# When twelve weight stores and one fraction are issued: chunked attention, Fourier mixing and an MLP in fp32

## The chip, the cores and the metric

The kernel runs on one core of a Trainium2 chip. Time is device time in microseconds from one execution; the median over runs is given. A core has five engines that work side by side: TensorE (matrix products, "PE"), VectorE ("DVE"), ScalarE ("ACT"), GpSimd ("POOL") and SyncE ("SP"), which here only issues transfers. Each engine takes its instructions in the order in which the program emits them and waits on semaphores for what other engines and transfers deliver.

## The reference

For 8 batches of 576 tokens and 8 heads of 64, attention is computed within chunks of 64 tokens; the heads are then joined to rows of 512, mixed with the real part of a two-dimensional Fourier transform, normalised, and sent through an MLP with 2048 hidden channels.

```python
scores = scale * np.matmul(q_c, k_c.transpose(0, 1, 2, 4, 3))   # per chunk of 64
attn = np.exp(scores - np.max(scores, axis=-1, keepdims=True))
attn = attn / (np.sum(attn, axis=-1, keepdims=True) + 1e-09)
out = np.matmul(attn, v_c)
x = out.transpose(0, 2, 1, 3).reshape(B, S, H * D)

X = np.fft.fft(np.fft.fft(x, axis=1), axis=2)
u = x + np.real(X).astype(np.float32)
un = (u - mean(u)) / np.sqrt(var(u) + 1e-06)                    # per row of 512
ch = np.maximum(un @ w_ch1, 0.0) @ w_ch2                        # 512 -> 2048 -> 512
return (u + ch).astype(np.float32)
```

q, k and v are float32. The two weights are float64 numbers, 8 bytes each.

## The kernel before

**Tiles and groups.** The tokens of a batch are cut into tiles of 128 rows (a low and a mirrored high tile per pair of chunks) and a rest. Four tiles of a batch make a group; the rests of all batches make the last. The kernel goes through the groups one by one: `mlp(g)` is the MLP of group g, and it yields after every small portion of matmuls. The main loop counts these steps as `t`. Between two steps it puts in portions of the attention and the Fourier mixing of the next batch (`side(b)`, spread over the steps between the times in `ready_at`), and everything else that has to be done by then. So the order of each engine's queue is that in which this loop emits instructions. Group 0 takes the steps 1 to 32: 16 steps up (512 to 2048, line 1219), and 16 down (2048 to 512, line 1260). From group 1 on, the products use fewer, precombined blocks (lines 1309 and 1363; the last two groups line 1427).

**Weights.** There are 32 pieces of 128x512 numbers: 16 of the first weight, into `wa`, and 16 of the second, into `wb`. A piece arrives as raw 8-byte numbers (512 KB, `load_weight`, line 348, issued on SP's queue) in one of a few raw spaces, which lie in `yall` and in rows of `xall`. Later on only three such spaces are left, so that a load waits until an earlier piece has been read. The conversion to float32 is written out by hand in `round_weight(i)`. It works on two pieces at once, the head of piece i and the tail of piece i - 1:

- head: VectorE takes the exponent bits (372) and the upper fraction bits (382). ScalarE makes the fraction, a number from 1 to 2 (`fraction`, line 364), and in two steps the power of two (`exponent` 367, `power_` 370).
- tail: VectorE adds the lower bits to the fraction (379), sets the sign on the power (380), and multiplies both (388). After 380 the raw space is free, and the next load is issued.

With `later` given, the three ScalarE steps are not emitted at once but put into a list, in the order fraction, exponent, power. Piece 1 is handled so: `fourier_early` calls `round_weight(1, put_off, "h")`, and `put_off[0]`, `[1]` and `[2]` are its three steps.

**The first rows.** `fourier_early` mixes the first batch. After the products of line 928 it emits the first two of the put-off steps. Then, for four tiles, VectorE adds the mixed rows (952, 955) and takes their statistics (705, 706). ScalarE makes the inverse deviation (709, 710), and for the first two tiles the normalised rows (996 to 998); VectorE makes those of the other two (1000). TensorE turns the rows (`turned`, line 399), ScalarE copies them to `unT` (1013), and `columns` multiplies them with piece 0 (944). The third put-off step stands after the second tile's turn. The first product with piece 1 is the first of line 1219.

**Stores for later groups.** Groups from 1 on read their weights from blocks kept in DRAM (`s1` and `s2`). Of the second weight, `keep2_whole(i)` stores three unchanged blocks of 256 KB each (line 1114, SP's queue, four calls, so twelve stores), and `keep2(i)` has GpSimd make four sums (line 1095), which go first into rows of `xall` or into `yall` and are stored from there (line 1107). The rows of `xall` are those of the raw spaces. Of the first weight, `keep1_store` (1082) stores blocks as well. All these stand in SP's queue with the loads of the weights and of q, k and v (252, 265, 275).

The loop emits the calls of `keep2_whole` when the pieces that they read have been converted (`n_w` is the number of the next piece):

```python
while n_whole < HF // 2 and n_w > KF + HF + 2 * n_whole + 2:
    keep2_whole(n_whole)
    n_whole += 1
```

Here KF is 16, HF is 8 and `ready_at[0]` is 27.

**The Fourier rows of batch 1** are made in the steps from 20 on (`fourier(1)`): products z on TensorE (722, 732), ScalarE's copies (747, 761), then `round_next()` and only after it `z_joined` on VectorE (752, 756), ScalarE's copies into `zf` (773 to 778), products `mix` (840), VectorE's sums (850, 851), the addition to x (857, on GpSimd for the high tiles), statistics, and the normalised and turned rows for group 1.

Of the kernel before, what the change touches and what calls it, by code (L numbers as in the profile page):

```python
# [11 lines left out]
ALU = mybir.AluOpType  # L12
# [4 lines left out]
def kernel(  # L17
# [32 lines left out]
    nc = tc.nc  # L50
# [10 lines left out]
    KF = DFF // 128  # L61
# [41 lines left out]
    NO, HF = 7, KF // 2  # L103
# [235 lines left out]
    def raw(i):  # L339
        return spaces[raws[i]].bitcast(U32).rearrange("p (f r) -> p f r", r=2)  # L340

    def load_weight(i):

        fit = [r for r in free if (i < N_EARLY or r < N_LATE) and (i < N_LAST or r > 1)]
        if i < len(pieces) and fit:
            raws[i] = fit[0]
            free.remove(fit[0])
            nc.sync.dma_start(out=raw(i).rearrange("p f r -> p (f r)"), in_=pieces[i][1].bitcast(U32))

    def round_weight(i, later=None, parts="ht"):  # L350

        head, tail = "h" in parts and i < len(pieces), "t" in parts and 0 < i <= len(pieces)
        if head:
            w, t = pieces[i][0], raw(i)
            hi, wi = t[:, :, 1], w.bitcast(U32)  # L360
            p = power[i] = three_p.tile([128, 512], U32, tag="o", name="power")

            def fraction(w=w, wi=wi):
                nc.scalar.activation(out=w, in_=wi, func=ACTF.Copy, scale=2.0 ** -20, bias=1.0)

            def exponent(p=p):
                nc.scalar.activation(out=p, in_=p, func=ACTF.Relu, scale=-1.0, bias=top[:, 0:1])

            def power_(p=p):
                nc.scalar.activation(out=p, in_=p, func=ACTF.Relu, scale=-8.0, bias=top[:, 1:2])  # L370

            nc.vector.tensor_scalar(p, hi, 0x7FF00000, None, ALU.bitwise_and)
            if later is None:
                exponent()
                power_()
        if tail:
            w_, t_ = pieces[i - 1][0], raw(i - 1)
            p_ = power.pop(i - 1)
            nc.vector.scalar_tensor_tensor(w_, t_[:, :, 0], 2.0 ** -52, w_, ALU.mult, ALU.add)
            nc.vector.scalar_tensor_tensor(p_, t_[:, :, 1], 0x80000000, p_, ALU.bitwise_and, ALU.bitwise_or)  # L380
        if head:
            nc.vector.tensor_scalar(wi, hi, 0x000FFFFF, None, ALU.bitwise_and)
            if later is None:
                fraction()
            else:
                later += [fraction, exponent, power_]
        if tail:
            nc.vector.tensor_tensor(out=w_, in0=w_, in1=p_.bitcast(FP32), op=ALU.mult)

            r = raws.pop(i - 1)  # L390
            if i - 1 + len(spaces) < N_EARLY or r < N_LATE:
                free.append(r)
            load_weight(max(raws, default=i - 1) + 1)
# [476 lines left out]
    def fourier_early():  # L870
# [59 lines left out]
                    start=(T == 0), stop=(T == 2), skip_group_check=True,  # L930
                )
        idle[0] = mid
        for do in put_off[:2]:
            do()
        keep_warm(3)
        yield
        ups = ps_a.tile([128, 2, 512], FP32, tag="att", name="up_a")
# [3 lines left out]
        def columns(s):  # L941

            for m, up in enumerate(first_ups):
                nc.tensor.matmul(
                    out=up[:, s * 128:(s + 1) * 128], lhsT=w1[:, 0, m * 128:(m + 1) * 128],
                    rhs=unTs[0][:, 0, s * 128:(s + 1) * 128], start=(s == 0), stop=False, skip_group_check=True,
                )

        for i in range(NM):
# [13 lines left out]
            if i == 0:  # L963
                normed(0, 1)
                turned(0, 0)
                keep_warm(1)
        put_off[2]()
        put_off.clear()
        columns(1)
        normed(0, 2)  # L970
# [109 lines left out]
    def keep1_store(pair, o):  # L1080
        to = s1[pair, o].rearrange("p (k x) -> p k x", k=2)
        nc.sync.dma_start(out=to, in_=parts1(pair)[o])
# [26 lines left out]
    def keep2_whole(i):  # L1109

        m = 2 * i
        to = s2.rearrange("o p (m e) -> o p m e", m=HF)
        for o, m0, e0 in ((0, m, 0), (4, HF + m, 0), (5, HF + m, HM)):
            nc.sync.dma_start(out=to[o, :, m:m + 2], in_=w2[:, m0:m0 + 2, e0:e0 + HM])
# [338 lines left out]
    def mlp(g):  # L1453

        for h1 in up_halves(g) if g >= first_of[1] else up_plain(g) if g > 0 else up_first():
            yield
        yield from (down_few if g >= FEW else down_halves if g >= first_of[2] else down_plain)(g, h1)

    with tc.manual_schedule():
# [22 lines left out]
        n_w = 2  # L1482
# [3 lines left out]
        def keep_warm(times):  # L1486

            for _ in range(times):
                nc.tensor.matmul(out=idle[0][:, 0:NQ], lhsT=warm[:, 0:128], rhs=warm[:, 0:NQ], start=True, stop=True)

        put_off, first_ups = [], []

        def round_next(later=None):
            nonlocal n_w
            if n_w <= len(pieces):
                round_weight(n_w, later)
                n_w += 1
# [25 lines left out]
        ready_at = [begin[g] + (2 * KF - 5 if g < first_of[2] else 2 * HF + 4) for g in range(NG)]  # L1523
# [12 lines left out]
        n_whole, n_kept, late, rest_ = 0, 0, [], None  # L1536
        conv2 = chain(conv2)
        t = 0
        for g in range(NG):
            for _ in mlp(g):  # L1540
                t += 1
                heavy = False
                for do in late:
                    do()
                late = []
                if t == 8:
                    nc.scalar.copy(tk, early_tk[:, :, :, 0:NE])
                if cur < len(sides):
                    t0 = 3 if cur == 0 else ready_at[cur - 1]
                    t1 = ready_at[cur]  # L1550
                    due = min(sizes[cur], (t - t0) * sizes[cur] // (t1 - t0))
                    if cur == 0:
                        due = late_due.get(t, (t - t0) * sizes[cur] // (t1 - 2 - t0))
                    while done < due:
                        heavy = next(sides[cur], None) or heavy
                        done += 1
                    if t >= t1:
                        for _ in sides[cur]:
                            pass
                        cur, done = cur + 1, 0  # L1560
                while joined:
                    combined(*joined.pop(0))
                if not heavy:
                    round_next(late if t < KF and t % 4 == 3 else None)
                    if t <= 2 or t < KF and t % 4 == 0 or t >= KF + 3:
                        round_next()

                while n_whole < HF // 2 and n_w > KF + HF + 2 * n_whole + 2:
                    keep2_whole(n_whole)
                    n_whole += 1  # L1570
                keep2_store()
                if n_w > len(pieces):
                    for _ in range(3):
                        next(conv2, None)
                if t == begin[1] - 1:
                    for _ in conv2:
                        pass
                    keep2_store()
                if begin[1] < t < begin[1] + 7 and t % 2:
                    keep1((t - begin[1] + 1) // 2)  # L1580
                if t == ready_at[FEW - 1]:
                    rest_ = make_rest()
                if t >= ready_at[FEW - 1]:
                    next(rest_, None)
                if t == begin[FEW] + 2 * HF - 2:
                    for _ in rest_:
                        pass
                    slab3.extend(
                        one_p.tile([128, Z3], FP32, tag=tag, name="more").rearrange("p (m e) -> p m e", m=4)
                        for tag in ("q", "k")  # L1590
                    )
                for _ in range((2, 3, 10, 11, 12, 12, 13, 13, 14, 15).count(t - begin[FEW])):
                    fetch(3)
                for _ in range(2 if t > begin[1] else 0):
                    if put_off:
                        b, t0_, r, o = put_off.pop(0)
                        nc.sync.dma_start(out=out[b, t0_ + 1 - r:t0_ + CH:2, :], in_=o)
                if KF < t <= KF + 4 or KF + 8 <= t < KF + 16:
                    keep1_store(n_kept // 3, (0, 4, 6)[n_kept % 3])
                    n_kept += 1  # L1600
                if begin[1] <= t < begin[1] + KF:
                    keep1_store((t - begin[1]) // 4, (2, 1, 3, 5)[(t - begin[1]) % 4])
                if t in (begin[1] + 9, begin[1] + 13, begin[1] + 16):
                    fetch(2)
                if t == begin[1] + KF:
                    for _ in range(NS1):
                        fetch(1)
# [49 lines left out]
```

## Time and profile before

| what | value |
|---|---|
| time, median of 3 runs | 1063.99 us (1063.61 to 1064.34) |
| profiled execution, its time | 1063.73 us |
| its span | 1061.9 us |
| TensorE busy | 1043.3 us (98%) |
| VectorE busy | 626.5 us (59%) |
| ScalarE busy | 315.5 us (30%) |
| GpSimd busy | 431.9 us (41%) |
| transfers | 219.10 MB, mean 206 GB/s |

The span is the part of the profiled execution between its first and its last instruction. Busy shares are averages over the whole kernel. What a stage is worth is read from the timeline of that stage: an engine's instructions in order of time, with the idle time before a group and what ended it. The chain of waits follows the work that ended last back to what released it, step by step. Where it names an engine other than TensorE, TensorE's work could not begin before that engine's.

### The profile page before, as it was taken

To read this page: it belongs to the slowest core of one execution; us is meant where nothing else is said; L and a number is where in the kernel's file an instruction comes from. 1 tells how busy PE (TensorE), PEld (TensorE's weight loads), DVE (VectorE), ACT (ScalarE), POOL (GpSimd) and SP (SyncE) were. 2 spreads that over 40 slices of the span, in tenths; PEclk is the share of its full clock that TensorE was granted. 3 is DMA by queue.
4 is the path that set the end of the run, shared out by engine and by line. 5 is a ranking of instruction groups with operands and counts; after the bars stand their busy time and mean duration, and the time that the engine had idled before them with its cause. 6 is when DMAs were issued, how large, how long until landed. Compare 5 with 4: busy or idle time off the path is not lost.

```text
span 1061.9 us, 20222 instructions
## 1 busy us (share of the span) xinstructions
PE 1043.3 (98%) x7482; PEld 851.6 (80%) x7482; DVE 626.5 (59%) x1339; ACT 315.5 (30%) x744; POOL 431.9 (41%) x555
## 2 busy tenths in 40 slices
PE   7999999999999999999999999999999999999998
PEld 6645444788888888888888888888888888888887
DVE  4798986974567465664565645745664666443332
ACT  4688573233113311332022312331133103201200
POOL 3410119753425151244134421514252777660282
PEclk9999999999999999999999999999999999999999
DMA  8767675687688447973678357944753759998364
GB/s 169 221 197 213 163 218 199 203 233 230 231 215 230 134 142 214 250 207 108 186 229 223 118 169 231 250 131 155 215 168 102 269 187 353 363 399 279 89 216 142
DMA packets 167088, 219.10 MB, mean 206 GB/s; under 512 B 77228, under 2 KB 111020, under 8 KB 161614
## 3 DMA queue, kind: packets, MB, share of 16 engines
q1 hardware_dynamic: 155978, 211.98, 64.8%
q0 software_dynamic: 9024, 4.91, 2.1%
q8 instruction: 60, 0.98, 0.4%
q10 hardware_dynamic: 1988, 0.92, 0.3%
q14 instruction: 38, 0.31, 0.1%
HBM read 183.61 MB, written 34.08 MB: 205 GB/s over the span
## 4 chain that ended last, share of the span: by engine, by line
PE 79%; DVE 6%; DMA 4%; ACT 3%; POOL 3%; SPq 2%; issue 2%; DVEq 0%; ACTq 0%; POOLq 0%
PE pa L1309 20%; PE pb L1309 15%; PE pb L1363 14%; PE pa L1363 11%; PE dn L1427 7%; PE pt L399 2%; SPq L265 2%; PE mix L840 2%; PE xp L501 2%; PE z L722 1%; DMA xall<-in_moe_w_ch_dram 1%; PE up L1219 1%; PE sc L451 1%; POOL h L1207 1%; POOL part L1156 1%
## 5 line engine op out<-in xcount | busy, mean ns | idle before, releaser
L1309 PE MATMUL pa<-unT,wa 128*128 128x256 f32 x736 | 175.3, 381 | 0.2 <-DVE xall L1317 0.2
L1309 PEld LDWEIGHTS pa<-unT,wa 128*128 128x128 f32 x736 | 138.1, 190 | 19.6 <-DVE xall L1317 0.6
L1309 PE MATMUL pb<-wa 128*128 128x256 f32 x448 | 106.6, 381 | 0.0
L1309 PEld LDWEIGHTS pb<-wa 128*128 128x128 f32 x448 | 84.3, 190 | 11.5
L1363 PE MATMUL pa<-wb,h 128*128 128x256 f32 x384 | 87.2, 380 | 0.0
L1363 PE MATMUL pb<-wb,h 128*128 128x256 f32 x384 | 86.4, 379 | 0.0
L1193 POOL TENSOR_TENSOR h<-h 128x256 f32<-128x256 f32 x48 | 40.8, 858 | 98.2 <-DVE wb L1191 91.6
L1363 PEld LDWEIGHTS pa<-wb,h 128*128 128x128 f32 x384 | 71.8, 190 | 9.7
L1363 PEld LDWEIGHTS pb<-wb,h 128*128 128x128 f32 x384 | 72.0, 190 | 9.4
L1044 POOL DMA_DIRECT2D out_dram<-wb x28 | 18.8, 674 | 121.8 <-DVE wb L1380 71.9
L1315 DVE TENSOR_TENSOR wa<-pb,wa 128x256 f32<-128x256 f32 x56 | 23.7, 424 | 63.5 <-ACT wa L1314 63.5
L1309 PE MATMUL pb<-unT,wa 128*128 128x256 f32 x256 | 60.6, 379 | 0.1
L1325 ACT ACTIVATE h<-pa 128x256 f32<-128x256 f32 x64 | 24.6, 384 | 115.0 <-PE pa L1309 114.1
L1260 PE MATMUL dn<-wb,h 128*128 128x512 f32 x128 | 58.7, 608 | 0.0
L1314 ACT COPY wa<-pa 128x256 f32<-128x256 f32 x56 | 20.9, 372 | 121.4 <-PE pa L1309 121.4
L1309 PEld LDWEIGHTS pb<-unT,wa 128*128 128x128 f32 x256 | 48.6, 190 | 7.1 <-DVE wa L1315 0.5
L1207 POOL TENSOR_TENSOR h<-h 128x512 f32<-128x512 f32 x34 | 42.8, 1276 | 27.2 <-ACT h L1331 24.1
L1309 PE MATMUL pa<-wa 128*128 128x256 f32 x224 | 53.9, 383 | 0.0
L483 ACT COPY pT<-pt 128x512 f32<-128x512 f32 x36 | 21.0, 582 | 105.8 <-PE pt L399 105.5
L1331 ACT ACTIVATE h<-h 128x512 f32<-128x512 f32 x64 | 40.0, 630 | 39.5 <-DVE h L1330 39.1
L1219 PE MATMUL up<-unT,wa 128*128 128x512 f32 x108 | 49.4, 598 | 0.0
L857 POOL TENSOR_TENSOR xall<-y,xall 128x513 f32<-128x513 f32 x14 | 22.3, 1590 | 61.1 <-DVE y L851 45.0
(312 smaller groups left out, 2136.6 us busy)
## 6 DMA issues: line engine op xcount, KB each, us to landing
wa<-s SPq DMA_DIRECT2D x196, 256.0 KB
wb<-s SPq DMA_DIRECT2D x42, 1024.0 KB
wb<-s SPq DMA_DIRECT2D x32, 512.0 KB
xall<-in_moe_w_ch_dram SPq DMA_DIRECT2D x22, 512.0 KB
q<-in_q_dram SPq DMA_DIRECT2D x96, 112.0 KB
k<-in_k_dram SPq DMA_DIRECT2D x96, 112.0 KB
s<-part SPq DMA_DIRECT2D x32, 256.0 KB
v<-in_v_dram SPq DMA_DIRECT2D x124, 64.0 KB
```

The lines of the kernel that those rows point to most:

```text
L265: eng.dma_start(out=t[p0:p0 + np_], in_=src[b, :, c * CH:c * CH + np_, :].rearrange("h p d -> p h d"))
L857: eng.tensor_tensor(out=x[:, 0:w], in0=y[:, 0:w], in1=x[:, 0:w], op=ALU.add)
L1193: nc.gpsimd.tensor_tensor(out=h1[:, m, hi], in0=h1[:, m, lo], in1=h1[:, m, hi], op=ALU.subtract)
L1207: eng.tensor_tensor(out=out_, in0=a, in1=b, op=op)
L1219: nc.tensor.matmul(out=up, lhsT=w1[:, kk, m * 128:(m + 1) * 128], rhs=unT[:, kk], start=(kk == 0), stop=(kk == KD - 1), skip_group_check=True,
L1260: nc.tensor.matmul(out=dn, lhsT=h1[:, m, s * 128:(s + 1) * 128], rhs=w2[:, m, :], start=(m == 0), stop=(m == KF - 1),)
L1309: nc.tensor.matmul(out=dst, lhsT=w[:, kk, r], rhs=rhs[o][:, kk], start=(o in (0, 1) and kk == 0), stop=(kk == 1), skip_group_check=True,)
L1315: nc.vector.tensor_tensor(out=b, in0=pbs[r][:, 0], in1=a, op=ALU.add)
L1325: nc.scalar.activation(out=h1[:, m, lo], in_=dst, func=ACTF.Relu)
L1331: nc.scalar.activation(out=h1[:, HF + m], in_=h1[:, HF + m], func=ACTF.Relu)
L1363: nc.tensor.matmul(out=dst, lhsT=lhs[:, m], rhs=w[:, m], start=(o in (0, 2) and m == 0), stop=(m == HF - 1), skip_group_check=True,)
L1427: nc.tensor.matmul(out=dst, lhsT=lhs[:, m], rhs=w[:, m], start=(fresh and not half and m == 0), stop=(m == 3), skip_group_check=True,)
```

## The change

Three edits, of which the first two belong together.

1. In `fourier_early`, the fraction of piece 1 is no longer emitted before the first normalised rows but after the third put-off step. On ScalarE, `fraction` (364) moves from ahead of `exponent` (367) to behind `power_` (370), which itself stands after the second tile's turn. Between its old place and its new one lie 18 ScalarE instructions: `exponent`, then those from the first 709 to `power_`.
2. In `round_weight(2)`, whose tail is that of piece 1, VectorE sets the sign on the power first and adds the lower bits to the fraction second. For all other pieces the order stays.
3. The calls of `keep2_whole` wait until `t > ready_at[0] - 4`, which is step 24, and then come one per step, at steps 24, 25, 26 and 27. The twelve stores stay the same. In SP's queue the order from the third-last load of a weight on was: load, three stores, one store of line 1082, two loads, nine stores, a store of 1082, four stores of sums in `xall`, two of 1082, four of sums in `yall`. It becomes: load, a store of 1082, two loads, three stores, a store of 1082, three stores, four of sums in `xall`, a store of 1082, three stores, a store of 1082, three stores, four of sums in `yall`, two of 1082.

The instructions of TensorE and GpSimd and their order stay the same.

```diff
@@ round_weight
         if tail:
             w_, t_ = pieces[i - 1][0], raw(i - 1)
             p_ = power.pop(i - 1)
-            nc.vector.scalar_tensor_tensor(w_, t_[:, :, 0], 2.0 ** -52, w_, ALU.mult, ALU.add)
-            nc.vector.scalar_tensor_tensor(p_, t_[:, :, 1], 0x80000000, p_, ALU.bitwise_and, ALU.bitwise_or)
+            for part in (1, 0) if i == 2 else (0, 1):
+                if part == 0:
+                    nc.vector.scalar_tensor_tensor(w_, t_[:, :, 0], 2.0 ** -52, w_, ALU.mult, ALU.add)
+                else:
+                    nc.vector.scalar_tensor_tensor(p_, t_[:, :, 1], 0x80000000, p_, ALU.bitwise_and, ALU.bitwise_or)
@@ fourier_early
         idle[0] = mid
-        for do in put_off[:2]:
-            do()
+        put_off[1]()
         keep_warm(3)
         yield
...
         put_off[2]()
+        put_off[0]()
         put_off.clear()
         columns(1)
@@ the main loop
-                while n_whole < HF // 2 and n_w > KF + HF + 2 * n_whole + 2:
+                if n_whole < HF // 2 and t > ready_at[0] - 4:
                     keep2_whole(n_whole)
                     n_whole += 1
                 keep2_store()
```

## The prediction

> **What bounds the kernel now.** The page of the profile comes first: TensorE is busy for 98% of the span and holds 79% of the chain that ended last, so a microsecond elsewhere counts only where TensorE waits for it. I therefore looked for its waits. The longest between 30 and 1057 us is at 152.8 us, and both parts of the change lie ahead of it. The chain of waits, asked for 130 to 205 us (columns: start, us, what), shows that TensorE hardly appears in it there:
>
> ```profile
> 136.86 4.52 DMA xall<-in_moe_w_ch_dram
> ...
> 143.06 6.75 DMA xall<-in_moe_w_ch_dram
> 149.83 0.43 DVE power L372
> ...
> 152.40 0.68 DVE zs L752
> ...
> 154.43 0.77 ACT zf L773 x2
> ...
> 159.85 1.48 POOL xall L1095
> ...
> 170.65 0.43 DVE y L851
> ```
>
> Two loads of weight pieces (512 KB each) head this chain. The first takes 4.5 us from its issue to its use, the second 6.75 us. Behind the second, VectorE's L372 holds up the joining of the Fourier rows (L752), because VectorE works in program order; then come ScalarE's copies into zf, GpSimd's sums, the normalised rows, and TensorE's transposes. Why the second load is slow is seen in the timeline of SP's queue (start, us over which the issues stretch, what, count):
>
> ```profile
> 136.86 3.53 SPq L348 DMA_DIRECT2D xall<-in_moe_w_ch_dram  x2
> 140.44 1.53 SPq L1114 DMA_DIRECT2D s<-wb  x3
> 142.02 0.63 SPq L1082 DMA_DIRECT2D s<-wa  x1
> 143.06 3.66 SPq L348 DMA_DIRECT2D xall<-in_moe_w_ch_dram  x2
> 146.77 14.62 SPq L1114 DMA_DIRECT2D s<-wb  x9
> ```
>
> Three stores of 256 KB (L1114) and one of L1082 were issued right ahead of the slow load. The next view is TensorE's timeline; the last bracket is the idle time before a group and who ended it:
>
> ```profile
> 155.25 0.49 PE L840 MATMUL mix<-ce,zf 128*128 128x129 f32 x2 [2.47 <-ACT zf L773]
> 156.83 4.91 PE L1260 MATMUL dn<-wb,h 128*128 128x512 f32 x8
> ...
> 171.21 0.63 PE L399 MATMUL pt<-ident,un 128*128 128x128 f32 x4 [0.40 <-DVE y L851]
> ...
> 175.81 0.63 PE L399 MATMUL pt<-ident,un 128*128 128x128 f32 x4 [0.53 <-DVE y L851]
> ```
>
> TensorE stands 2.47 us for zf, and its next eight matmuls take 4.91 us where the same group takes 3.60 at 162.68. The stretches tell why (busy us per engine, then granted clock, DMA share, GB/s):
>
> ```profile
> 146.00:150.00 4.00, 4.00 (x10) 1.71 (x9) 1.46 (x4) 2.74 (x8) 0.00 (x0) 1.00 1.05 374
> 156.00:159.50 3.50, 3.50 (x8) 1.84 (x7) 3.07 (x3) 3.12 (x10) 2.54 (x2) 0.51 0.04 13
> ```
>
> DMA runs full at 374 GB/s while the load is under way, and after the stall the clock is halved for some 3.4 us. That loss is not on the chain: TensorE arrives at 171.21 and still waits 0.40. ScalarE's timeline shows the other place:
>
> ```profile
> 42.42 0.63 ACT L364 ACTIVATE wa<-wa 128x512 f32<-128x512 uint32 x1
> 42.94 0.72 ACT L367 ACTIVATE power<-power,top 128x512 uint32<-128x512 uint32 x1
> 43.55 0.29 ACT L709 ACTIVATE rstd<-st,eps 128x1 f32<-128x1 f32 x1
> ...
> 48.74 0.71 ACT L370 ACTIVATE power<-power,top 128x512 uint32<-128x512 uint32 x1
> 50.09 1.07 ACT L1013 COPY unT<-pt 128x512 f32<-128x512 f32 x2 [0.64 <-PE pt L399]
> ```
>
> L364 and L367 belong to weight piece 1 and stand before the first normalisation (L709); after L370 there is a gap of 0.64 us.
>
> **What the Trainium skill says.** "DMA: Bandwidth & Descriptors", section "Queues, rings and completion order": on each DMA engine the descriptors of one ring are consumed in ring order. The trace agrees: the load behind four stores needed 6.75 us, the one at 136.86, behind one store, 4.5. "TensorE: Matmul & The Clock Gate", section "Part 1: The HAM clock gate": a free-running window of about 3.4 us with little TensorE work halves the clock. The trace agrees (0.51 over 3.5 us after the 2.47 us gap); the 1.14 us gap at 181.24 halved nothing. Same page, "Architectural detail": ScalarE and VectorE work strictly first in, first out; the order in both timelines is that of the program.
>
> **Part 1, the fraction on ScalarE.** L364 leaves from before L367. L367 can start at 42.42, and L709 when L367 lets it, at about 43.03: earlier by L364's pitch, 0.52 us. Its statistics are ready, since VectorE's L706 ends at 42.80. The following ScalarE steps come back to back, and their VectorE inputs (45.91 and 47.50 for the third and fourth rows) are ready in time, so all move up by about 0.5. L364 now runs after L370: 48.2 to 48.9 is L370, 48.8 to 49.45 L364, and TensorE's transposes free the third unT copy (50.09 before) at 49.57. So the gap covers it, by 0.1 us; without that cover it costs up to 0.6 us. VectorE then reads power (L380) before the fraction (L379): swapped, so L379 begins about 49.75, after L364 has ended. Piece 1 is done at 51.4 instead of 51.88, and the first matmul that reads it comes at 52.1 instead of 52.62. No DMA is moved. Between: gain 0 (all absorbed by 143 us) and 0.52. TensorE is nearly gapless from 52 to 152 us, and the loads are released by VectorE, which moves along, so I take 0.5.
>
> **Part 2, the stores.** Twelve stores (L1114, 3 MB) stay as many; each group of three waits for step 24 and then one group per step. In SP's order the three at 140.44 move behind the last two loads, and of the nine at 146.77 three stay ahead of the four xall stores (L1107) and six go behind them. So ahead of the load of 143.06 only L1082 remains. The three loads before it needed 4.02 (134.38 to 138.40), 4.55 and 4.69 us (140.03 to 144.72), a mean of 4.42: it would be in use at 147.48 instead of 149.83, a gain of 2.35. Bounds: VectorE is busy until about 147.0, so at most 2.8; nothing, if the load was slow for another reason. I take 2.3.
>
> What follows: VectorE needs 2.49 us from L372 to L752, so L752 starts at 149.97 (ScalarE's zs copy ends at 148.84, in time). zf comes at 152.9 where TensorE's previous group ends at 152.77: stall and halved clock go. The last load, issued about 146.3, lands by some 150.7, before VectorE wants it at 151.5. The last piece's L380 ends at 157.4 instead of 159.77, GpSimd's four sums and L857 follow, and the transposes of 171.21 become possible at 168.9. Late next is this very chain: TensorE, unslowed, arrives at 152.9 + 1.10 + 3.43 + (170.81 - 161.58) = 166.7 and now stalls 2.2 us there. So of some 4 us that TensorE wins, 2.3 remain. From there VectorE's, ScalarE's and GpSimd's chain to 201 us has the same lengths and starts 2.3 earlier; after it TensorE is dense to the end.
>
> Sum on the profiled execution: 1063.73 - 2.3 - 0.5 = 1060.93 (its span 1061.9, 1.83 around it). It lies 0.26 under the median of the runs, 1063.99; so 1061.2.
>
> **Rivals.**
> (a) The start's half microsecond is swallowed before 143 us, by a landing or by L364 colliding with the unT copy; stores as forecast: 1063.99 - 2.3 = 1061.7. For it: 0.1 us of cover.
> (b) The stall that moves to 166.7 costs a halved clock on the chain. 3.4 us at half speed lose 1.7 us; TensorE's slack behind it is 0.53 at 175.81 and 0.1 at 180.59, so up to 1.1 is lost, more if a landing takes some of the 2.3 too: about 1062.7. For it: 2.2 us is close to the 2.47 that halved it before. Against: the 1.14 did not, and the window must contain the whole gap.
> (c) The load isn't faster, as reads need 4 to 4.7 us even without stores ahead and the lone store ahead may hold it as well; only 0.5 is won: 1063.5.
> (d) Slower: SP works in order, and the six stores behind the xall stores (which wait for GpSimd until about 161) delay the yall stores, the third batch of sums and then the q and k loads; a k load (191.60, 4.01 us) is on the chain. Those six are 1.5 MB, 4.2 us at the 363 GB/s of 162 to 166 us; SP would finish by about 172, and is next wanted at 181.01 - 2.8 = 178.2. From 6 us of delay each us costs one; slower by 0.2% needs 6 + 2.8 + 2.1 = 11 us. At 12 us, 1066.5.
>
> **How the numbers follow.** 0.2% is 2.1 us, about what a measurement of this kernel tells from no change; the line is 1061.86. Chances: forecast 0.50, (a) 0.14, (b) 0.18, (c) 0.10, (d) 0.08. Faster: nearly all of the forecast and most of (a), together 0.62. Within: the rest of those, (b) and (c), 0.31. Slower: 0.07. The fastest end is both upper bounds, 2.8 + 0.52, and the 0.7 us by which the runs shown spread: 1060.0; the slow end takes in (c) with half that spread: 1063.9. The forecast's own range is 1060.4 to 1061.8.
>
> **What would show it** (line numbers of before; most stand three lower in the changed file). Right: L709 first at about 43.0; the first matmul of piece 1 at 52.1; no L1114 between the last four loads; the 30th piece's L372 waiting for its DMA under 1 us and starting near 147; no gap of 2 us before mix at 153, but one of about 2 us before the first transposes of the second group, near 168.4; the first L1309 near 188.6 instead of 191.39. Wrong: that load still over 6 us; a half clock after 168 with later transposes; SP issuing q loads past 182; or the difference at 201 us not reaching the end of the span.

## The result, and the profile after

| | kernel before | kernel after |
|---|---|---|
| median of this comparison | 1063.8 us (7 runs, 1062.93 to 1064.76) | 1060.65 us (7 runs, 1059.34 to 1061.4) |
| ratio, 95% interval | | 0.9967 [0.9958, 0.9977] |
| profiled execution, its span | 1063.73 us, 1061.9 us | 1060.87 us, 1059.1 us |

The kernel became faster by 3.5 us (0.33%). Line numbers of the changed kernel are mostly three higher than before: L364, L367, L370 and L372 stay; L379 and L380 are L381 and L383, L752 is L755, L1114 is L1117, L1309 is L1312. In the kernels of the experiments they can differ by one from these.

Executions of one kernel differ by up to a microsecond before the changed code begins. So I set the two profiles against each other at the first product named `mid` ahead of the first normalised rows, which the change does not touch: at 42.72 us before (42.99 in a second execution), at 42.00 after (41.52 in a second). Times given as "after mid" below are counted from there.

The timeline of SP's queue in the kernel after (start, us over which the issues stretch, what, count) shows the third edit:

```profile
135.63 3.47 SPq L348 DMA_DIRECT2D xall<-in_moe_w_ch_dram  x2
139.16 0.52 SPq L1085 DMA_DIRECT2D s<-wa  x1
141.99 3.13 SPq L348 DMA_DIRECT2D xall<-in_moe_w_ch_dram  x2
145.17 1.54 SPq L1117 DMA_DIRECT2D s<-wb  x3
```

No L1117 stands between the last loads any more. The chain of waits of the kernel after (start, us, what) has these answers to the lines of before:

```profile
135.63 4.68 DMA xall<-in_moe_w_ch_dram
...
141.99 3.80 DMA xall<-in_moe_w_ch_dram
145.81 0.43 DVE power L372
...
148.38 0.68 DVE zs L755
...
150.41 0.78 ACT zf L776 x2
...
155.83 1.48 POOL xall L1098
```

The load that took 6.75 us from issue to use takes 3.80. Everything behind it, down to GpSimd's sums, is some 4 us earlier, 0.72 us of which is the execution's own earlier start. TensorE's timeline of the kernel after (the last bracket is the idle time before a group and who ended it):

```profile
151.39 0.39 PE L843 MATMUL mix<-ce,zf 128*128 128x129 f32 x2
...
152.49 3.60 PE L1263 MATMUL dn<-wb,h 128*128 128x512 f32 x8
...
167.19 0.93 PE L402 MATMUL pt<-ident,un 128*128 128x128 f32 x4 [2.04 <-DVE y L854]
167.91 5.04 PE L1263 MATMUL dn<-wb,h 128*128 128x512 f32 x8
...
178.35 0.66 PE L402 MATMUL pt<-ident,un 128*128 128x128 f32 x4 [0.27 <-ACT unT L1016]
```

The stall of 2.47 us ahead of `mix` is gone, and the eight products behind it take 3.60 us. A stall of 2.04 us stands ahead of the transposes of the second group instead, and now the group behind that one takes 5.04 us. ScalarE's timeline of the kernel after shows the first edit:

```profile
41.70 0.72 ACT L367 ACTIVATE power<-power,top 128x512 uint32<-128x512 uint32 x1
42.32 0.29 ACT L712 ACTIVATE rstd<-st,eps 128x1 f32<-128x1 f32 x1
...
47.50 0.71 ACT L370 ACTIVATE power<-power,top 128x512 uint32<-128x512 uint32 x1
48.12 0.62 ACT L364 ACTIVATE wa<-wa 128x512 f32<-128x512 uint32 x1
48.85 1.07 ACT L1016 COPY unT<-pt 128x512 f32<-128x512 f32 x2
```

L712 comes straight behind L367, and L364 ends at 48.74, 0.11 us before the copy L1016 begins.

**Where the time went.** After mid, the first product of line 1312 stands at 145.36 us, where that of line 1309 stood at 148.67: 3.31 us earlier. The last product of the span is only 2.02 us earlier (1012.54 against 1014.56). The 1.3 us between are given back late, between 906 and 933 us of the kernel before. Matched product by product, 0.6 us of them are lost at 923.91 us of the kernel after, where TensorE waits for a block of weights from DRAM; the rest goes in steps of 0.1 to 0.3 us around it. TensorE's timeline after:

```profile
923.91 3.69 PE L1430 MATMUL dn<-xall,h 128*128 128x256 f32 x16 [0.42 <-DMA xall<-s]
...
930.12 1.97 PE L1430 MATMUL dn<-more,yall 128*128 128x256 f32 x8 [0.51 <-DVE wb L1440]
```

A wait like the one at 930.12 stands in the kernel before as well (0.42 us at 932.89).

### The profile page after: what moved, and what is told of

Read it like the earlier page. It is cut to its first block, busy times and chain, and to the rows that moved or that the text cites. A ratio compares the mean times of both kernels' runs of the same rounds, so it can differ in the third digit from the quotient of the medians.

```text
span 1059.1 us, 20224 instructions
## 1 busy us (share of the span) xinstructions
PE 1043.6 (99%) x7482; PEld 852.3 (80%) x7482; DVE 627.7 (59%) x1339; ACT 314.4 (30%) x744; POOL 433.2 (41%) x555
## 4 chain that ended last, share of the span: by engine, by line
PE 80%; DVE 7%; ACT 4%; DMA 4%; SPq 3%; issue 2%; POOL 1%; DVEq 0%; ACTq 0%; POOLq 0%
PE pa L1312 20%; PE pb L1312 15%; PE pb L1366 15%; PE pa L1366 12%; PE dn L1430 8%; PE pt L402 2%; PE mix L843 2%; PE xp L504 2%; PE z L725 1%; SPq L265 1%; DMA xall<-in_moe_w_ch_dram 1%; PE sc L454 1%; DVE power L383 1%; DMA xall<-s 1%; DVE wb L381 1%
## 5 line engine op out<-in xcount | busy, mean ns | idle before, releaser
L1312 PE MATMUL pa<-unT,wa 128*128 128x256 f32 x736 | 175.4, 381 | 0.2 <-DVE xall L1320 0.2
L1312 PEld LDWEIGHTS pa<-unT,wa 128*128 128x128 f32 x736 | 138.0, 190 | 19.8 <-DVE xall L1320 0.6
L1312 PE MATMUL pb<-wa 128*128 128x256 f32 x448 | 106.6, 381 | 0.0
L1312 PEld LDWEIGHTS pb<-wa 128*128 128x128 f32 x448 | 84.3, 190 | 11.5
L1312 PE MATMUL pb<-unT,wa 128*128 128x256 f32 x256 | 60.6, 379 | 0.2 <-DVE wa L1318 0.2
L1312 PEld LDWEIGHTS pb<-unT,wa 128*128 128x128 f32 x256 | 48.6, 190 | 7.1 <-DVE wa L1318 0.6
L1312 PE MATMUL pa<-wa 128*128 128x256 f32 x224 | 53.9, 383 | 0.0
L860 POOL TENSOR_TENSOR xall<-y,xall 128x513 f32<-128x513 f32 x14 | 22.2, 1588 | 61.1 <-DVE y L854 45.0
```

The costliest lines, as they stand in the source:

```text
L860: eng.tensor_tensor(out=x[:, 0:w], in0=y[:, 0:w], in1=x[:, 0:w], op=ALU.add)
L1312: nc.tensor.matmul(out=dst, lhsT=w[:, kk, r], rhs=rhs[o][:, kk], start=(o in (0, 1) and kk == 0), stop=(kk == 1), skip_group_check=True,)
```

## The experiments

Theory: the two parts work side by side, the later stores gain some 2.3 us because a load no longer queues behind three of them, and the moved fraction gains its pitch of 0.5 us. Rivals: the gain comes from the order of all twelve stores, or from what they collide with later; the fraction's part is swallowed; the half clock that moved along decides.

**The kernel before, looked at again,** tells how far one execution differs from another.

> The kernel before once more, unchanged, for a second profile. If the differences between profiles ahead of the first normalised rows (0.7 us) and in the wait for transferred blocks near 930 us (1.2 us) are of the execution and not of the change, both differ from the first profile of before by amounts of that size; the stall of 2.5 us before the first mixed rows and the 6.8 us of the load are there again.

Measured: span 1063.3 us. After mid, `mix` at 112.64 (before 112.53), the first L1309 at 148.79 (148.67). Up to there the two agree to 0.12 us. From L1309 to the last product they take 866.79 and 865.89 us. So the late wait differs by 0.9 us between executions of one kernel.

**The stores alone.**

```diff
-                while n_whole < HF // 2 and n_w > KF + HF + 2 * n_whole + 2:
+                if n_whole < HF // 2 and t > ready_at[0] - 4:
```

> The later stores alone, the fraction where it was before. Theory (the load behind the stores heads a chain that does not involve TensorE, and its whole gain is carried to the end): the last load but one is in use 2.3 to 2.8 us earlier after the start of its own issue, VectorE no longer waits for it, and the time falls by 2.3 to 2.8 us, ratio 0.9974 to 0.9978. Rival (the gain needs both parts, as the half microsecond of the start makes the landings fit): under 1.5 us. Rival (the load was slow for another reason): 0.

Measured: 0.998 [0.9972, 0.9987], 2.1 us; `mix` at 110.14 after mid, L1309 at 146.28, so 2.4 us earlier than before at both. VectorE's timeline of the kernel before has the use of piece 30, the piece of the slow load:

```profile
149.83 0.43 DVE L372 TENSOR_SCALAR power<-xall 128x512 uint32<-128x512 uint32 x1 [2.54 <-DMA xall<-in_moe_w_ch_dram]
```

The timeline of this kernel (uses of pieces 28 to 30, counted from 0):

```profile
141.96 0.43 DVE L372 TENSOR_SCALAR power<-xall 128x512 uint32<-128x512 uint32 x1 [1.04 <-DMA xall<-in_moe_w_ch_dram]
144.45 0.42 DVE L372 TENSOR_SCALAR power<-xall 128x512 uint32<-128x512 uint32 x1
147.29 0.43 DVE L372 TENSOR_SCALAR power<-xall 128x512 uint32<-128x512 uint32 x1 [0.29 <-DMA xall<-in_moe_w_ch_dram]
```

The bracket of 2.54 us is down to 0.29. The longest wait is now that of piece 28, two loads earlier.

**Only the first three stores held back,** all others as before.

```diff
-                while n_whole < HF // 2 and n_w > KF + HF + 2 * n_whole + 2:
+                while n_whole < HF // 2 and t > 20 and n_w > KF + HF + 2 * n_whole + 2:
```

> Before, with only the first three of the twelve stores moved behind the last two loads; the nine others stay ahead of the stores of sums, the fraction stays. Theory (only the three stores ahead of the load matter, because the transfers of one queue are taken in order): the same gain as the later stores alone, 2.3 to 2.8 us. Rival (the nine stores behind the loads matter too, by traffic or by holding up the stores of sums): about half of it or less.

Measured: 0.9977 [0.9968, 0.9987]; `mix` at 110.39 after mid, L1309 at 146.55. That is the stores' whole effect within the scatter. The nine others, one group per step or all at once, are neither its cause nor its price.

**The same three stores from GpSimd's queue,** with the loop as before.

```diff
-            nc.sync.dma_start(out=to[o, :, m:m + 2], in_=w2[:, m0:m0 + 2, e0:e0 + HM])
+            (nc.gpsimd if i == 0 else nc.sync).dma_start(out=to[o, :, m:m + 2], in_=w2[:, m0:m0 + 2, e0:e0 + HM])
```

> Before, with the three stores ahead of the last two loads issued at the same place of the program, but from GpSimd's queue, which stands idle there for 28 us. The bytes are moved at the same time, only not in SP's order. Theory (what delays the load is the order within one queue): the load is in use 1.3 to 2.8 us earlier, and the time falls by 1.3 to 2.8 us, ratio 0.9974 to 0.9988. Rival (it is the bytes of that moment, whatever the queue): the load is as late as before, ratio 1.000.

Measured: 0.9982 [0.9972, 0.9991]; `mix` at 110.60, L1309 at 146.75, 1.9 us earlier than before. SP's timeline:

```profile
140.07 0.52 SPq L1082 DMA_DIRECT2D s<-wa  x1
142.63 4.01 SPq L348 DMA_DIRECT2D xall<-in_moe_w_ch_dram  x2
```

The load is in use at 147.28, 4.65 us after its issue, with no wait of VectorE for it. But order and moment are not told apart by this. GpSimd, which had nothing else to do, issued the first store at 126.93 us and the other two at 137.50, where SP had issued all three from 140.44 on, and their packets had all begun by 142.88, when the load had just been issued. So the bytes were not moved at the time of before, although the expectation says so.

**Order, seen in the packets.** What this run leaves open, the traces of the others show, since they record every packet (the piece in which a transfer is moved) with its start, its size and its queue. The stores of blocks have packets of 1 KB, the loads of weights 4 KB. In the kernel before, the four stores ahead of the slow load are 1024 packets of 1 KB, which begin between 143.33 and 148.16 us. The load is issued at 143.06, but from 144.22 to 146.91 not one packet of 4 KB begins: the load's first one (the last two loads are the last 256 packets of that size) comes 3.85 us after its issue, when 869 of the 1024 have begun. A second execution has 3.08 us there, the kernel with the fraction alone 3.36. In the eight kernels and executions whose only store ahead is the one of L1082, the first packet comes 0.97 to 1.04 us after the issue. This is order within one queue, and it is worth 2 to 3 us.

**Six stores ahead instead of three: the first three sent twice,** with the same data to the same place.

```diff
                     keep2_whole(n_whole)
+                    if n_whole == 0:
+                        keep2_whole(0)
                     n_whole += 1
```

> Before, with the three stores ahead of the last two loads issued twice (768 KB more, same data to the same place). Theory (what lies ahead in the queue is paid in full): at 374 GB/s 768 KB are 2.1 us, so VectorE gets the load 2.1 us later, about 8.8 us after its issue, TensorE's stall before the first mixed rows grows from 2.5 to 4.6 us, and the time rises by 2.1 us, ratio 1.0020. Rival (the slow load has another cause, reads of that moment): no change of its time beyond 0.5 us, ratio 1.0000.

Measured: 1.0044 [1.003, 1.0059], 4.7 us slower (4 runs) where 2.1 were expected; `mix` at 116.34 after mid, 3.8 us later than before. SP's timeline shows that this is not the case that was meant:

```profile
140.35 7.11 SPq L1114 DMA_DIRECT2D s<-wb  x6
147.52 0.52 SPq L1082 DMA_DIRECT2D s<-wa  x1
148.13 1.09 SPq L348 DMA_DIRECT2D xall<-in_moe_w_ch_dram  x2
```

SP itself stood. The waits of SP's queue between 138 and 150 us (engine, line, what it waited for; us in total, times, longest) name what for:

```profile
SPq L1114 <- DMA s<-wb: 4.3, 3, 3.9
```

The second three waited for stores, up to 3.9 us, and the load behind them was issued 5.3 us later after mid. By then it needed 5.30 us to its use. The trace names the semaphores: the three repeated stores wait, one after the other, for 107, 108 and 109, which the three stores to the same blocks signal when they are done. The three added stores of the next kernel, which go elsewhere, have no such wait.

**Six stores ahead, the added three to memory that nothing reads,** so that none waits for another.

```diff
             nc.sync.dma_start(out=to[o, :, m:m + 2], in_=w2[:, m0:m0 + 2, e0:e0 + HM])
+        if i == 0:
+            to = spare.rearrange("o p (m e) -> o p m e", m=HF)
+            for o, m0, e0 in ((0, m, 0), (4, HF + m, 0), (5, HF + m, HM)):
+                nc.sync.dma_start(out=to[o, :, m:m + 2], in_=w2[:, m0:m0 + 2, e0:e0 + HM])
```

> The kernel before with three more stores of 256 KB ahead of the slow load, of the same data to memory that nothing reads, so that no store waits for another. The three issues take 1.5 us; SP had some 0.4 us to spare ahead of the load of 143.06, so that load is issued about 1.1 us later. Theory that a load queues behind the stores ahead of it, 2.3 us for three: in use 6.8 to 9.1 us after its issue, mix and the first L1309 2.3 to 3.5 us later than before, time 1.0022 to 1.0033 of it. Rival, that only the issue counts and the bytes ahead cost nothing: in use 6.8 us or less after its issue, mix 1.1 us later at most, time 1.0010 or less.

Measured: 1.0028 [1.002, 1.0035], 3.0 us slower; `mix` at 115.84 after mid, 3.3 us later, L1309 at 151.99, also 3.3. SP's timeline:

```profile
139.61 1.53 SPq L1115 DMA_DIRECT2D s<-wb  x3
141.19 2.41 SPq L1119 DMA_DIRECT2D spare<-wb  x3
143.65 0.52 SPq L1083 DMA_DIRECT2D s<-wa  x1
144.27 1.21 SPq L349 DMA_DIRECT2D xall<-in_moe_w_ch_dram  x2
```

VectorE's timeline of the same kernel has the use of that load:

```profile
152.14 0.43 DVE L373 TENSOR_SCALAR power<-xall 128x512 uint32<-128x512 uint32 x1 [6.23 <-DMA xall<-in_moe_w_ch_dram]
```

In use 7.87 us after its issue, where it took 6.77 behind three stores: three stores more cost 1.1 us behind the issue, and 2.2 us because the load is issued later (102.56 after mid instead of 100.34). The theory's sum of 2.3 to 3.5 us holds, and the rival of at most 1.1 us falls; but two thirds of the price of these three is paid at SP's issue and one third behind it.

**The fraction alone** (edits 1 and 2, the loop of the stores as before; the diff is that of the change without its last part).

> The fraction of piece 1 behind the normalised rows (with the swapped pair on VectorE) alone, the stores as before. Theory (ScalarE's rows move up by one pitch of the activation, and VectorE's loads and conversions with them): the first transposes of normalised rows come 0.5 us earlier relative to the products before them, the same half microsecond stands at 143 us and at 201 us, and the time falls by 0.5 us, ratio 0.9995. Rival (the load behind the stores swallows it, since its landing is set by the queue): 0 at 201 us, ratio 1.0000.

Measured: 1.0000 [0.9988, 1.0011], so neither an effect nor the expected 0.9995 can be told. The profile is finer. After mid:

| us after mid | before | again | fraction alone | stores alone | after | after, again |
|---|---|---|---|---|---|---|
| first transposes of normalised rows | 2.68 | 2.68 | 2.15 | 2.67 | 2.16 | 2.16 |
| first product with piece 1 | 9.89 | 9.90 | 9.37 | 9.89 | 9.37 | 9.38 |
| issue of the fifth load from the last | 91.66 | 91.65 | 91.17 | 91.64 | 91.15 | 91.15 |
| `mix` | 112.53 | 112.64 | 112.35 | 110.14 | 109.38 | 109.42 |
| first L1309 or L1312 | 148.67 | 148.79 | 148.51 | 146.28 | 145.36 | 145.58 |

The edit is worth 0.52 us at the first transposes and still 0.5 at 91 us, in each execution of the table that has it and in none that has it not. From there to `mix` only 0.2 to 0.3 us of it are left with the old stores. The chain there runs through landings of loads (the one issued at 93.6 to 94.2 took 4.55 us to its use before and 5.06 here), and these scatter by half a microsecond.

**VectorE's old order for piece 1's tail,** the rest as in the changed kernel.

```diff
-            for part in (1, 0) if i == 2 else (0, 1):
+            for part in (0, 1):
```

> The changed kernel with VectorE's old order in the tail of piece 1: lower bits first, then the sign. Theory (the cover of the moved fraction is 0.7 us at the first product with piece 1, and VectorE waits 0.86 us for ScalarE a few instructions later): VectorE waits about 0.35 us for the fraction, TensorE's first product with piece 1 stays where it is, and the time is that of the changed kernel, ratio to before 0.997. Rival (the swap is what makes the fraction's move pay): the half microsecond of the start is gone, ratio 0.9975.

Measured: 0.9971 [0.9962, 0.998], as the changed kernel. L381, the first reader of the moved fraction, waits a little in VectorE's timeline:

```profile
51.66 0.69 DVE L381 SCALAR_TENSOR_TENSOR wa<-yall,wa 128x512 f32<-128x512 uint32 x1 [0.25 <-ACT wa L364]
```

The first product with piece 1 comes at 9.37 after mid all the same. The swap is not needed.

**The changed kernel again, and what now sets the end.** After the change, the transposes at 167.19 wait for VectorE's L854. Its row is made after the statistics of the tile before, and that tile's addition, L860 on GpSimd, begins only at 160.46, behind five sums of line 1098. So three of those sums were put behind that addition (fewer sums in step 23, none in step 24, more in step 25: "the sums later"); and in another kernel four sums were moved into the time ahead, when GpSimd is idle ("the sums split").

```diff
-                    for _ in range(3):
+                    for _ in range({23: 2, 24: 0, 25: 5}.get(t, 3)):
```

> The changed kernel with one more move, of program order alone: of GpSimd's sums of the second weight only two are emitted at step 23, none at step 24 and five at step 25, so that the addition of the mixed rows to the first high tile stands behind two sums instead of five. Theory (the chain to the transposes of group 1 runs over GpSimd's queue, and TensorE stands 2.0 us at its end): the addition starts about 3 us earlier, when VectorE's y is ready; TensorE, which comes at 165.2, waits no longer, so the transposes come about 2 us earlier and the time falls by 2.0 us, to about 1058.6 where the changed kernel has 1060.65; ratio to before about 0.995. Rival (the sums put off are late next and hold up the stores, the combined blocks or group 1's first products): no gain over the changed kernel, ratio 0.997, or slower.

Measured: 0.9974 [0.9961, 0.9988], no better than the changed kernel. The profile shows both halves. TensorE's timeline:

```profile
164.98 0.60 PE L402 MATMUL pt<-ident,un 128*128 128x128 f32 x4
...
185.11 0.70 PE L454 MATMUL sc<-kT,qT 64*64 64x64 f32 x32 [0.86 <-DVE kT L421]
185.74 1.99 PE L1312 MATMUL pb<-xall,wb 128*128 128x256 f32 x8
```

The transposes do come without a wait, 1.8 us earlier after mid, but L1312 only by 1.2. A new wait stands at 185.11 for VectorE. This profile's span was 1056.4 us, 2.7 under the changed kernel's, so it was run again with the changed kernel beside it.

> The changed kernel, unchanged, on one chip with the two kernels below. Expected: 0.997 of the kernel before, profiled span 1058.5 to 1060.5 us, first L1312 about 145.4 us after the first product of the middle matrix (197.44 - 10.07 - 42.00 = 145.37), at 187.4.

> The changed kernel with GpSimd's first sums of group 1's second half put behind the last piece's share. Theory that the chain from the last weight piece through GpSimd to the transposes is what now sets the end, and that half of the gain is lost again to sums that run later beside VectorE: L1312 1.2 us earlier than in the changed kernel, 0.5 us left at the end, so 0.5 us (0.05%) under it. Rival, that a profile's 2.7 us lower span is due to this edit: 1.5 us or more (0.15%) under it.

Measured: the changed kernel 0.9976 [0.9969, 0.9983], span 1059.0 us; the sums later 0.9982 [0.9974, 0.999], span 1062.1 us. L1312 is 1.9 us earlier this time (143.71 against 145.58 after mid), and the span 3 us longer: from L1312 to the last product it takes 871.18 us, in the first execution 866.01. Of the first profile's 2.7 us, 1.2 stand at L1312, as much again comes from the late part and 0.4 from the start. So the edit does bring L1312 forward, but the late part's scatter is larger than what it brings. Neither the expected 0.05% nor the rival's 0.15% is seen.

```diff
-        conv2 = iter([keep2(1), keep2(0), first_sums(), keep2(3), keep2(2)])
+        conv2 = iter([keep2(2), keep2(1), keep2(0), first_sums(), keep2(3)])
...
-                    for _ in range(3):
+                    for _ in range({23: 7, 24: 0, 25: 5}.get(t, 3)):
```

> The same, but four of the sums that were late now run in GpSimd's idle stretch at 147.7 to 152.8 us, so that GpSimd ends its sums some 5 us earlier. Theory that VectorE's copies of turned rows are slowed by GpSimd's sums running beside them (1.4 us instead of 0.4 us each): the last of them before L1312 take 0.4 us, and L1312 comes 1 to 2 us earlier than with the sums merely later; in time 1 to 2.5 us (0.1 to 0.25%) under the changed kernel. Rival, that the early sums slow VectorE's conversion of the last pieces in return: mix up to 1 us later and no gain. Rival, that VectorE's copies wait for something else: they still take 1.4 us.

Measured: 0.9968 [0.9954, 0.9983], from 6 runs; not told apart from the changed kernel. L1312 comes at 145.69 after mid: no gain. VectorE's timeline of the changed kernel has, beside an idle GpSimd:

```profile
126.28 0.69 DVE L576 TENSOR_TENSOR sum<-xall 128x512 f32<-128x512 f32 x1 [0.28 <-POOL sum L575]
```

VectorE's timeline with the sums split shows the theory right and the gain lost ahead of it:

```profile
126.44 1.77 DVE L576 TENSOR_TENSOR sum<-xall 128x512 f32<-128x512 f32 x1 [0.28 <-POOL sum L575]
...
151.13 1.26 DVE L372 TENSOR_SCALAR power<-xall 128x512 uint32<-128x512 uint32 x1
152.31 1.77 DVE L381 SCALAR_TENSOR_TENSOR wb<-xall,wb 128x512 f32<-128x512 uint32 x1
...
156.62 1.75 DVE L381 SCALAR_TENSOR_TENSOR wb<-xall,wb 128x512 f32<-128x512 uint32 x1
...
181.53 1.49 DVE L1036 TENSOR_TENSOR unT<-unT 128x256 f32<-128x256 f32 x1
182.94 0.41 DVE L1034 TENSOR_TENSOR xall<-unT 128x256 f32<-128x256 f32 x1
183.39 0.43 DVE L1035 TENSOR_TENSOR xall<-unT,xall 128x256 f32<-128x256 f32 x1
183.73 0.42 DVE L1036 TENSOR_TENSOR unT<-unT 128x256 f32<-128x256 f32 x1
```

GpSimd's timeline of the same kernel:

```profile
126.39 1.26 POOL L1098 TENSOR_TENSOR yall<-wb 128x512 f32<-128x512 f32 x1
...
181.29 1.45 POOL L1098 TENSOR_TENSOR xall<-wb,xall 128x512 f32<-128x512 f32 x1
```

What the expectation calls copies of turned rows (L1034 to L1036) are differences of two blocks each. The second and third take 1.4 to 1.5 us while GpSimd adds, and all take 0.4 us as soon as GpSimd's last sum has ended at 182.74. So the theory holds. But the moved sums cost VectorE time in two earlier places. The first of them came as early as 126.39, beside VectorE's L576, which then took 1.77 us instead of 0.69; VectorE and the loads that it releases were 1.06 us later from there on (fifth load from the last at 92.21 after mid instead of 91.15), and 0.3 to 0.8 us of it are left at `mix` (110.17 after mid). The others ran from 149.61 to 153.53, beside the conversion of the last pieces: L372 took 1.26 us where the changed kernel has 0.42, the next L381 1.77 instead of 0.68, and from the last L759 to the first L853 VectorE needed 9.06 us instead of 6.93. These 2.1 us are the larger loss, and they are just what the rival said: early sums slow the conversion of the last pieces.

## Why the prediction was right

The sum gave 1060.93 us for a profiled execution, 1061.2 for the median; the profile gave 1060.87, the medians 1060.65 and, in the later comparison, 1061.36. That the single profile agrees to 0.06 us is luck: the difference of 2.8 us in the span is, but for rounding, 3.3 us gained at the first L1312, where 2.8 were forecast, 1.3 given back after 906 us, and 0.7 by which this execution began earlier for no reason of the change. The step-by-step claims:

- *L709 at about 43.0, the first matmul of piece 1 at 52.1, 0.1 us of cover.* 42.32, 51.38 and 0.11, with this execution's 0.72 earlier start: 43.04 and 52.10. As forecast. The reordering on VectorE, which the working used to keep L379 behind L364, makes no difference.
- *0.5 us for the start, all of it carried on.* Carried exactly to the loads at 91 us after mid; then the landings decide. Alone it left 0.2 to 0.3 us at `mix`. With the new stores, five executions that have both parts (after, after again, the old order, and both with later sums) have `mix` at 109.38 to 109.84 after mid, mean 109.54 (the sums split, with its late loads, is left out); three with the new place of the first stores alone have 110.14 to 110.60, mean 110.38: 0.8 us. The 0.5 lies between, and no run settles it better. Rival (a) was the description of what the single execution of this part shows.
- *The load in use 4.42 us after its issue, a gain of 2.3 us, at most 2.8.* Against the two profiles of before, at 112.53 and 112.64, `mix` gains 1.9 to 2.5 us by the stores alone: the term is right in size. Its parts are not: the use came 3.6 to 3.8 us after the issue with the first stores moved on SP's queue and the sums in place, so some 3 us sooner than before, but in two kernels without the fraction's part (the stores alone, and the first three held back) the issue itself came 0.7 and 1.0 us later. In the profile after, the use came 3.82 us after the issue, without a wait of its own on VectorE's side beyond 0.1 us, so there it reached the bound given. What the step left out is that the bound is not VectorE alone. Once the slow load is quick, the loads ahead of it head the chain: in every execution with the new order VectorE still waits 0.2 to 1.4 us for at least two of the three before it, and their scatter of half a microsecond is that of the gain.
- *Why the load was slow.* The order within a queue (the ring order that the prediction took from the Trainium skill) is right: the load's first packet began 3.1 to 3.9 us after its issue behind the three stores, and 1 us after it without them. What the prediction did not count is that stores also hold up SP's issue. For the three that the change moves this was small: the load went out at 100.34 after mid before, at 99.99 and 100.38 in the changed kernel. For three stores more it was 2.2 of 3.3 us.
- *Stall and halved clock at 153 go, a stall of 2.2 us comes before the transposes.* 2.04 us at 167.19, as forecast (168.4 less the 0.72 of the start and the 0.5 that the load gained beyond 2.3).
- *L1309 at 188.6.* 187.37; with the same two differences, 188.6.
- *The difference at 201 us reaches the end.* Not shown right. In the profile 1.3 us of 3.3 are given back between 906 and 933 us. The stretch from L1309 to the last product took 865.89 and 866.79 us before, 867.18, 867.33 and 867.13 in the three executions with the changed order of work, 865.64 to 866.80 in those with one part alone. An earlier start does not by itself make this stretch longer: the kernel with three stores more, whose L1309 comes 3.3 us later than before, took 867.13 us as well, and the sums later took 866.01 and 871.18. So scatter can explain it, though so few executions do not prove it. The first ratio, 3.5 us, says that it costs little; the second, 2.6 us, leaves room for it.
- *Rival (b), the halved clock after the moved stall.* It came, in the profile after: 5.04 instead of 3.60 us. The argument against it, that a window must contain the whole gap, is nearly right for a gap of this length (last section), but here one did. The changed kernel again, in the same view, has the stall and no halved clock (line numbers one lower):

```profile
166.92 0.63 PE L401 MATMUL pt<-ident,un 128*128 128x128 f32 x4 [2.10 <-DVE y L853]
167.38 3.60 PE L1262 MATMUL dn<-wb,h 128*128 128x512 f32 x8
171.51 0.63 PE L401 MATMUL pt<-ident,un 128*128 128x128 f32 x4 [0.53 <-DVE y L853]
...
178.09 0.66 PE L401 MATMUL pt<-ident,un 128*128 128x128 f32 x4 [1.14 <-ACT unT L1015]
```

  From the first transposes to L1312 it takes 20.17 us with the halved clock and 20.18 without. So it costs nothing, and the price of up to 1.1 us that the prediction put on it was wrong. The step that failed is TensorE's slack: it was summed as 0.53 and 0.1 us, and the wait of 1.14 us that comes next, which the prediction itself names for another purpose, was left out. With it the slack is 1.77 us, and the halved clock had TensorE 1.69 us later at the end of that group.
- *Rival (c)* fell with the stores alone. *Rival (d):* SP's last early L1117 and L1110 are out by 167 us, and the q loads start at 180.42 us, where they started at 184.45 before: SP was never late.

## What to carry to other kernels

When a consumer waits for a load, read the queue ahead of it: what stands there can cost the load both its turn and its issue. Moving it behind the last load that somebody waits for was free here, because the queue has an idle stretch later. Before you price what comes next, add up all of an engine's waits up to the point where the chains meet; a wait left out turns a harmless loss into a feared one. Before you call a sum "off the critical path", look at what runs beside it. And a change of a few tenths of a microsecond is visible in a profile against a fixed early event long before it is in a median.

## What the runs showed of the hardware

- **VectorE beside GpSimd.** The same two-input subtraction of 128x256 numbers on VectorE takes 0.41 to 0.43 us alone and mostly 1.37 to 1.49 us while GpSimd runs its sums; an addition of 128x512 takes 0.69 and 1.77. The Trainium skill states the rule ("SBUF — State Buffer", section "Who interferes with whom": a VectorE instruction with two inputs in SBUF and a GpSimd instruction that reads SBUF exclude each other), and these traces agree. L372, which has one input, took 1.26 us instead of 0.42 beside a sum as well; no run here shows why. What I had not expected is where it bites: sums that are off the critical path set the pace of operations that are on it, and moved out of their way they met the next ones.
- **Whether a stall of 2 us halves the clock depends on where it falls.** Each trace records when the granted clock changes, and within a trace these times lie whole multiples of 3.413 us apart (before: 5.86, 156.05, 159.46 and 1060.58 us, so 44, 1 and 264 of them). That is the free-running window that the prediction cites, and it shows where every window of the execution begins. Six executions have a stall of 2.04 to 2.10 us ahead of the transposes:

| execution | stall, us | windows that it falls into begin at, us | without a matmul in each, us | next eight products, us |
|---|---|---|---|---|
| stores alone | 166.59 to 168.68 | 166.56 | 2.10 | 5.30, halved |
| after | 165.16 to 167.19 | 163.96 | 2.04 | 5.04, halved |
| first three held back | 166.59 to 168.69 | 163.27, 166.68 | 0.09, 2.01 | 3.60 |
| after, again | 164.82 to 166.92 | 161.90, 165.32 | 0.50, 1.60 | 3.60 |
| old order | 168.62 to 170.71 | 165.90, 169.31 | 0.70, 1.40 | 3.60 |
| from GpSimd's queue | 166.57 to 168.67 | 164.03, 167.44 | 0.87, 1.23 | 3.60 |

  Over all fourteen traces, from 60 us on, each of the 16 whole windows that ran at the full clock with 2.04 us or more without a matmul was followed by a halved one, and none of those with 2.01 us or less was. All five stalls ahead of `mix` (2.47 to 6.27 us) left at least 2.15 us of one window idle and were followed by a halved group of 4.75 to 5.54 us. The cited section speaks of an idle window; here some 60% of one is enough, and the measurement decides. In the first 60 us, where other forms of matmul run, one window with 1.86 us was followed by a halved clock too (old order, at 8.9 us). As the windows start anew at another point in each execution, the same stall in the same kernel is halved once and once not.
- **SP can stand in its stores.** An engine that only issues is held up by transfers: it stood up to 3.9 us with six stores of which three write what the others wrote, and the three stores to unused memory took 2.41 us to issue where three take 1.53.
